# Four loads in flight, x of step 3 on the DMA crossbar and no last decay columns, in a fused HGRN2 and feed-forward kernel

## Chip, cores and metric

One core of a Trainium2 chip. The metric is the device time of one execution in microseconds (us). A kernel is run several times; an execution is called slow when it lies more than 1.5% above the fastest of its kernel, and comparisons use the fast ones. Times here vary by some 2 us from run to run, so small differences are read from ratios with their 95% interval. Different chips are not compared by their times. The granted clock is the share of TensorE's full clock that the chip granted: 1.0 is full, 0.5 half.

## The reference

```python
# q, k, v, f_logit: (batch 4, heads 8, seq 768, head_dim 48)
f = 1 / (1 + exp(-f_logit))
for t in range(768):
    state = f[:, :, t, :, None] * state + outer(k[:, :, t], v[:, :, t])
    y[:, :, t] = q[:, :, t] @ state
x = y.transpose(0, 2, 1, 3).reshape(3072, 384)
out = (maximum(x @ w_gate, 0) * (x @ w_val)) @ w_out     # d_ff = 1536
```

## The kernel before

The sequence is cut into 6 steps of 128 positions, numbered 0 to 5; each step has four batches, handled in two pairs. Every pair needs four loads of 384 KB (f, k, q, v). From f, ACT makes the logarithm of the gate (exp at L572, ln at L575), and TensorE (PE) sums it over positions with a triangular matrix, the **cumulative matmul** L582. What follows (exp, products, transposes, scores) gives y, which is the x of the feed-forward part. That part is a large heap of matmuls (L766, L789), used as filler wherever the attention part has nothing for PE.

The order of all this is not written down by hand. Every operation is entered in a plan with an assumed duration, and a list scheduler walks through assumed time and appends to one queue per engine. The queues are fixed when the kernel is built, and each engine works through its own strictly in order.

```python
flight = 3
first_xbar_x = 4
...
def load(n, c, b0, b1, after=(), ...):
    flow = 0.9 * (b1 - b0)          # assumed transfer time: 1.8 us for a pair
    op = add("SP", lambda: e.dma_start(dst, src), ..., after=after)
    dma(op, ..., flow, 2.0)         # assumed to land: flow + 2.0 us, plus backlog
...
# each load depends on the one `flight` places before it, in the plan
# and, as a semaphore wait for its landing, in the kernel
loads.append(load(n, c, b, b + load_batches, loads[-flight:][:1]))
...
def cum():                          # L582, and four one-column matmuls L584
    te.matmul(bc.ap[:, 0:HD], tri[:, :], bn[:, :, 0:D])
    for p in range(NP):             # decay columns, for the state update
        mm = te.matmul(bc.ap[:, HD + p:HD + p + 1], bn[...], ones[:, :])
...
if c < first_xbar_x:                # x transposed by PE (L699), copied by DVE (L703)
    chain("transpose_x", "PE", transpose_x, ..., occ=0.2)
else:                               # x transposed by a DMA on the SP queue (L707)
    op = add("SP", lambda: sy.dma_start(xT[...], xn[ni][:, :], transpose=True), ...)
```

## Time and profile before

| | before |
|---|---|
| time, median of 3 runs | 203.14 us (202.06 to 204.03) |
| profiled span | 201.4 us |
| granted TensorE clock, mean | 0.992 |
| last f landed / cumulative matmul started | 127.3 / 129.76 us |

Most of the profile's lines are in the prediction. Three more are needed for the comparison: groups of instructions of the kernel before that wait for a load. The columns are line, engine, operation, operands, count; busy us and mean ns; then the idle time of the engine just ahead of these instructions and what ended most of it.

```profile
L605 POOL TENSOR_TENSOR hats<-q_in,expo 128x384 bf16<-128x384 f32 x20 | 20.0, 1002 | 2.2 <-DMA q_in<-in_q_dram 2.2
L558 POOL CAST vpad<-v_in 128x384 bf16<-128x384 f32 x24 | 12.0, 515 | 3.0 <-DMA v_in<-in_v_dram 2.8
L572 ACT ACTIVATE f_in<-f_in 128x768 f32<-128x768 f32 x10 | 8.4, 838 | 6.4 <-DMA f_in<-in_f_logit_dram 6.4
```

ACT stood 6.4 us in all waiting for f, POOL 5 us for q and v. PE hid nearly all of that behind filler.

### The profile page before, as it was taken

What the parts mean: (1) busy time and instruction counts of PE and PEld (TensorE: products, weight loads), DVE (VectorE), ACT (ScalarE), POOL (GpSimd) and SP (SyncE); (2) the same over time, 40 slices, a digit from 0 to 9 for tenths busy, and PEclk for the clock granted to TensorE, in tenths of its full rate; (3) what the DMA queues carried; (4) which work ended last, traced back from release to release, by engine and by line L of the source; (5) the groups of instructions that cost most, each with busy time, mean ns of one, the idle gap of its engine ahead of it and who ended that gap; (6) DMA issues with size and microseconds to landing.
All of it is one profiled execution on the core that took longest, in us unless ns stands there. A gap on an engine that the chain in (4) does not pass through costs nothing.

```text
span 201.4 us, 4570 instructions
## 1 busy us (share of the span) xinstructions
PE 191.7 (95%) x1813; PEld 124.4 (62%) x1813; DVE 107.9 (54%) x212; ACT 115.2 (57%) x264; POOL 77.3 (38%) x111
## 2 busy tenths in 40 slices
PE   7989899799999999999999999599999999999995
PEld 5766688676789787855664655245555555444564
DVE  7268575565098988628586846135462334433210
ACT  2976868716678686877677572744354333443412
POOL 5189203563559687772858364053000000000000
PEclk9999999999999999999999999969999999999999
DMA  4999999999999999999989998979222001111113
GB/s 119 234 223 196 198 200 180 204 231 210 230 232 232 158 247 189 221 198 230 192 161 234 159 199 186 189 156 221 77 63 59 24 19 39 39 39 42 39 39 117
DMA packets 116660, 31.35 MB, mean 156 GB/s; under 512 B 109600, under 2 KB 116640, under 8 KB 116640
## 3 DMA queue, kind: packets, MB, share of 16 engines
q1 hardware_dynamic: 112656, 27.53, 67.2%
q0 software_dynamic: 3984, 3.54, 11.0%
q8 instruction: 14, 0.23, 0.5%
q14 instruction: 6, 0.05, 0.1%
HBM read 25.95 MB, written 4.72 MB: 152 GB/s over the span
## 4 chain that ended last, share of the span: by engine, by line
PE 73%; DMA 13%; SPq 8%; ACT 2%; POOL 2%; issue 1%; DVE 0%
PE ps L766 37%; PE ps L789 22%; SPq L399 7%; DMA q_in<-in_q_dram 4%; DMA wv<-in_moe_w_val_dram 4%; PE ps L638 3%; DMA f_in<-in_f_logit_dram 3%; DMA v_in<-in_v_dram 3%; PE ps L615 2%; PE ps L677 2%; PE ps L582 2%; PE ps L673 2%; PE ps L718 1%; PE ps L699 1%; PE ps L584 1%
## 5 line engine op out<-in xcount | busy, mean ns | idle before, releaser
L777 DVE TENSOR_TENSOR gT<-relu,ps 128x256 bf16<-128x256 bf16 (+1 forms) x96 | 52.2, 552 | 59.9 <-PE ps L766 37.2
L766 PE MATMUL ps<-xT,wg 128*128 128x256 bf16 (+1 forms) x288 | 63.1, 328 | 0.3 <-DMA wg<-in_moe_w_gate_dram 0.3
L773 ACT ACTIVATE relu<-ps 128x256 bf16<-128x256 f32 (+1 forms) x96 | 46.3, 490 | 29.1 <-PE ps L766 28.7
L766 PE MATMUL ps<-xT,wv 128*128 128x256 bf16 (+1 forms) x288 | 62.6, 326 | 0.0
L789 PE MATMUL ps<-wo,gT 128*128 128x384 bf16 (+2 forms) x300 | 52.5, 320 | 0.0
L789 PEld LDWEIGHTS ps<-wo,gT 128*128 128x128 bf16 x300 | 27.7, 98 | 17.4
L766 PEld LDWEIGHTS ps<-xT,wg 128*128 128x128 bf16 x288 | 27.0, 98 | 15.6 <-DMA wg<-in_moe_w_gate_dram 0.6
L644 DVE TENSOR_TENSOR ptm<-ps,tri 128x512 bf16<-128x512 f32 x48 | 30.6, 684 | 10.8 <-PE ps L638 10.7
L766 PEld LDWEIGHTS ps<-xT,wv 128*128 128x128 bf16 x288 | 26.1, 98 | 16.0 <-ACT relu L773 0.2
L809 ACT ACTIVATE osb<-ps 128x384 f32<-128x384 f32 (+2 forms) x25 | 11.8, 477 | 30.6 <-PE ps L789 30.5
L602 POOL TENSOR_TENSOR hats<-k_in,expo 128x384 bf16<-128x384 f32 x20 | 20.0, 1000 | 20.3 <-ACT expo L591 20.3
L605 POOL TENSOR_TENSOR hats<-q_in,expo 128x384 bf16<-128x384 f32 x20 | 20.0, 1002 | 2.2 <-DMA q_in<-in_q_dram 2.2
L734 POOL TENSOR_TENSOR st<-ssum,dec 128x384 bf16<-128x384 f32 x16 | 13.3, 830 | 16.2 <-DVE ssum L732 16.2
L455 PE MATMUL ps<-zeros 128*128 128x256 bf16 x89 | 13.0, 301 | 1.1 <-DVE zeros L359 1.1
L691 ACT ACTIVATE xn<-ps 128x384 bf16<-128x384 f32 x20 | 9.8, 488 | 7.1 <-PE ps L677 7.1
L558 POOL CAST vpad<-v_in 128x384 bf16<-128x384 f32 x24 | 12.0, 515 | 3.0 <-DMA v_in<-in_v_dram 2.8
L572 ACT ACTIVATE f_in<-f_in 128x768 f32<-128x768 f32 x10 | 8.4, 838 | 6.4 <-DMA f_in<-in_f_logit_dram 6.4
L591 ACT ACTIVATE expo<-ps 128x384 f32<-128x384 f32 x20 | 9.8, 492 | 3.0 <-PE ps L584 2.9
L455 PEld LDWEIGHTS ps<-zeros 128*128 128x128 bf16 x89 | 9.0, 107 | 3.0 <-DVE zeros L359 1.1
L638 PE MATMUL ps<-qkT 48*128 48x128 bf16 x192 | 8.9, 226 | 1.2 <-ACT qkT L528 0.8
L593 ACT ACTIVATE expo<-ps 128x384 f32<-128x384 f32 x20 | 10.0, 498 | 0.0
L732 DVE TENSOR_TENSOR ssum<-ps,st 128x384 f32<-128x384 f32 x16 | 8.8, 551 | 1.1 <-PE ps L718 0.9
(71 smaller groups left out, 158.3 us busy)
## 6 DMA issues: line engine op xcount, KB each, us to landing
out_dram<-osb SPq DMA_DIRECT2D x23, 192.0 KB, 2.2
f_in<-in_f_logit_dram SPq DMA_DIRECT2D x10, 384.0 KB, 6.2
k_in<-in_k_dram SPq DMA_DIRECT2D x10, 384.0 KB, 6.4
q_in<-in_q_dram SPq DMA_DIRECT2D x10, 384.0 KB, 4.5
v_in<-in_v_dram SPq DMA_DIRECT2D x10, 384.0 KB, 4.8
wg<-in_moe_w_gate_dram POOLq DMA_DIRECT2D x3, 384.0 KB, 7.1
wv<-in_moe_w_val_dram POOLq DMA_DIRECT2D x3, 384.0 KB, 7.4
wo<-in_moe_w_out_dram POOLq DMA_DIRECT2D x3, 384.0 KB, 7.2
```

Source lines behind the costliest of these rows:

```text
L399: op = add(eng, lambda: e.dma_start(dst, src), [], [f"{n}{c % NL}_{b}" for b in range(b0, b1)], occ=(0.8 if eng == "SP" else 0.3) * (b1 - ...
L455: op = add("PE", lambda: te.matmul(cold.ap[:, 0:256], zeros[:, 0:128], zeros[:, :]), ["zeros"], [cold], occ=0.22 if i < 17 else 0.11, lat= ...
L558: add("POOL", lambda: gp.tensor_copy(vout, vin[:, b, :, :].rearrange("p (n j) d -> p n j d", j=2)), [f"v{li}_{b}", f"vpad{vi}"], [f"v_{vi} ...
L602: add("POOL", lambda: gp.tensor_tensor(hk, kin[:, b, :, :], ex[:, 1, :].rearrange("p (h d) -> p h d", h=H), ALU.mult), [f"k{li}_{b}", f"ex ...
L605: add("POOL", lambda: gp.tensor_tensor(hq, qin[:, b, :, :], ex[:, 0, :].rearrange("p (h d) -> p h d", h=H), ALU.mult), [f"q{li}_{b}", f"ex ...
L638: mm = te.matmul(s.ap[:, p * C:(p + 1) * C], qkT[qi][lo:lo + D, 1, p, :], qkT[qi][lo:lo + D, 0, p, :])
L644: add("DVE", lambda j=j, s=s: ve.tensor_tensor(ptm[mi][:, j, :, :], s.ap[:, :].rearrange("p (n t) -> p n t", n=NP), mask, ALU.mult), [s, " ...
L734: add("POOL", lambda: gp.tensor_tensor(t4(s_new), t4(tmp), rate, ALU.mult), [key] + dk, [f"S{b}_{c % 2}"], prio=P + 8, **pool_t(HD))
L766: mm = te.matmul(bank.ap[:, 0:n], wt[:, kt, j * 128:(j + 1) * 128], xT[xi][:, kt, n0:n1], start=(kt == 0), stop=(kt == NK - 1))
L773: add("ACT", lambda: sc.activation(relu[ri][:, 0:n], gate.ap[:, 0:n], AF.Relu), [gate], [f"relu{ri}"], prio=P, **act_t(n))
L777: add("DVE", lambda: ve.tensor_tensor(gT[gi][:, j, n0:n1], relu[ri][:, 0:n], val.ap[:, 0:n], ALU.mult), [val, f"relu{ri}"], [f"gT{gi}_{j}_ ...
L789: mm = te.matmul(o.ap[:, 0:n1 - n0], gT[gi][:, j, b * C:(b + 1) * C], wo[:, j, n0:n1], start=(j == 0), stop=(j == NJ - 1))
```

## The change

Its intent: let a fourth load be queued so that DMA never pauses; take the x transposes of one more step off PE, the full engine, and give them to the DMA crossbar; drop matmuls whose result nobody reads in the last step. The core of the diff (new knobs for the stores, which keep their old setting, are cut):

```diff
-    flight = 3
+    flight = 4
...
-    first_xbar_x = 4
+    first_xbar_x = 3
...
-                te.matmul(bc.ap[:, 0:HD], tri[:, :], bn[:, :, 0:D])
-                for p in range(NP):
+                mm = te.matmul(bc.ap[:, 0:HD], tri[:, :], bn[:, :, 0:D])
+                for p in range(NP if c < NC - 1 else 0):
...
-            chain("cum", "PE", cum, ..., occ=0.29, lat=PE_L,
+            chain("cum", "PE", cum, ..., occ=0.29 - (0.12 if c == NC - 1 else 0), lat=PE_L,
```

In the changed kernel nearly all the lines named here have a number one higher (L582 becomes L583).

More of the change, by code (lines that the diff above doesn't have):

```diff
@@ L253, in bass_hgrn2_outer__then__ffn_reglu_kernel @@
     n_tiled = 1
-    first_xbar_x = 4
+    first_xbar_x = 3
     load_batches = 2
     hat_engines = ['DVE', 'POOL']
+    STORE = 'SP'
     TAIL = [0, 256, 384]
@@ L586, in cum @@
                 return mm
-            chain("cum", "PE", cum, ["tri", "ones", f"bneg{bi}", f"bn{bi}_{bj}"], [bc], occ=0.29, lat=PE_L,
+            chain("cum", "PE", cum, ["tri", "ones", f"bneg{bi}", f"bn{bi}_{bj}"], [bc], occ=0.29 - (0.12 if c == NC - 1 else 0), lat=PE_L,
                 prio=P, opens=[bc])
@@ L811, in ffn_out @@
             dst = bass.AP(tensor=out.tensor, offset=(b * S + g * C) * DM + n0, ap=[[DM, C], [1, n1 - n0]])
-            op = add("SP", lambda dst=dst, oi=oi, n0=n0, n1=n1: sy.dma_start(dst, osb[oi][:, n0:n1]), [f"osb{oi}_{x}" for x in TAIL[:-1] if n0 <= x < n1], [f"out{g}_{b}_{n0}"],
-                     occ=0.2, lat=0.9, prio=P)
+            op = add(STORE, lambda dst=dst, oi=oi, n0=n0, n1=n1: (sy if STORE == "SP" else sc).dma_start(dst, osb[oi][:, n0:n1]), [f"osb{oi}_{x}" for x in TAIL[:-1] if n0 <= x < n1], [f"out{g}_{b}_{n0}"],
+                     follows=first_stores if g == 0 else [], occ=0.2 if STORE == "SP" else 0.4, lat=0.9 if STORE == "SP" else 1.2, prio=P)
             dma(op, f"osb{oi}_{n0}", 0.45 * (n1 - n0) / DM)
+    first_stores = [tails["loadSP"]] if '0' == "1" else []
     OJ = 4
@@ L864, in bass_hgrn2_outer__then__ffn_reglu_kernel @@
             op.val = n
-    stores = [op for op in order["SP"] if op.writes and op.writes[0].startswith("out")]
+    stores = [op for op in order[STORE] if op.writes and isinstance(op.writes[0], str) and op.writes[0].startswith("out")]
     def run(name, eng):
```

## The prediction

> **What bounds the kernel now.** I read the page first, then the chain that ended last in order of time, the timeline of TensorE (PE) and of the SP queue, and the SP queue's own waits.
>
> ```profile
> PE 191.7 (95%) x1813; PEld 124.4 (62%) x1813; DVE 107.9 (54%) x212; ACT 115.2 (57%) x264; POOL 77.3 (38%) x111
> PE   7989899799999999999999999599999999999995
> PEclk9999999999999999999999999969999999999999
> DMA  4999999999999999999989998979222001111113
> ```
>
> PE is full except for one slice (126 to 131 us); the next slices show a lowered clock. The DMA engines are full up to about 140 us and nearly idle after. So there are two regimes: up to 140 us loads and PE run neck and neck, and after it PE alone works off the feed-forward backlog. PE executes in order, so whatever it loses before 140 us is added to the end. The chain says what it lost:
>
> ```profile
> 119.42 1.22 SPq L812
> 120.68 1.19 SPq L707
> 121.92 5.33 DMA f_in<-in_f_logit_dram
> 127.27 0.84 ACT f_in L572
> ...
> 128.98 0.74 ACT bneg L575
> 129.76 0.34 PE ps L582
> ```
>
> This is f of the last step, second batch pair. It is issued behind a store and an x transpose, takes 5.33 us, and ACT needs 2.5 us from landing until the cumulative matmul L582 may start. PE's timeline shows the price:
>
> ```profile
> 126.76 0.81 PE L789 MATMUL ps<-wo,gT 128*128 128x384 bf16 x4
> 129.76 0.34 PE L582 MATMUL ps<-bneg,tri 128*128 128x384 bf16 x1 [2.19 <-ACT bneg L575]
> ...
> 131.99 1.44 PE L766 MATMUL ps<-xT,wg 128*128 128x512 bf16 x3
> ...
> 135.73 0.81 PE L766 MATMUL ps<-xT,wv 128*128 128x512 bf16 x3
> ```
>
> 2.2 us idle, and then the same three matmuls take 1.44 instead of 0.81 us. The table of windows gives a granted clock of 0.50 for 131.2 to 134.5, so about 1.65 us more are lost. Together 3.85 us is what better loading could win here.
>
> **What the Trainium skill says.** (1) "TensorE: Matmul & The Clock Gate", section "What's actually happening": the clock is at half or full speed, decided by a free-running window of about 3.4 us; an idle one halves it. The trace agrees in size (0.50 for some 3.3 us), though here the idle part was only 2.2 us. (2) Same page, "Back-to-back issue gap": N/2.4 + 2.5 ns for a warm matmul. For N = 128 that is 56 ns; the three L699 transposes below start 0.17 us before the next group: it agrees. (3) "Advanced Engine Details and Errata", "X-Bar Transpose (TRN2)": transposes by DMA are as fast as regular DMAs. This trace disagrees for the queue: an unobstructed x transpose of 96 KB holds SP for 1.24 us, a load of 384 KB for 0.45.
>
> ```profile
> 62.53 0.33 PE L699 MATMUL ps<-ident,xn 128*128 128x128 bf16 x3
> 62.70 0.49 PE L766 MATMUL ps<-xT,wv 128*128 128x256 bf16 x3
> ```
> ```profile
> 130.35 0.45 SPq L399 DMA_DIRECT2D q_in<-in_q_dram  x1
> 143.15 2.48 SPq L707 DMA_TRANSPOSE xT<-xn  x2
> ```
>
> **The change part by part.**
>
> Decay columns: 4 works x 4 one-column matmuls L584 go. A group of four takes 0.10 us from its start to the next group's (51.66 to 51.77), so 4 x 0.10 = 0.4 us of PE.
>
> x of step 3: 4 groups of L699 go, 4 x 0.17 = 0.7 us of PE, and four DVE copies L703 of 0.354 us, which are off the path. Sum on PE: **1.1 us**, certain. In exchange four DMA transposes enter the SP queue while it is contended.
>
> Flight: the load that stands `flight` places earlier is handed over as a true dependency, so each load waits for that one to land. What three in flight cost is in the SP queue's waits:
>
> ```profile
> SPq L399 <- DMA v_in<-in_v_dram: 0.5, 1, 0.5
> SPq L399 <- DMA q_in<-in_q_dram: 0.4, 1, 0.4
> SPq L399 <- DMA k_in<-in_k_dram: 0.4, 1, 0.4
> ```
>
> 1.3 us in all, near 64 to 70 us. After 76 us loads wait for no such landing. They take 1.5 to 2.9 us to issue when others are ahead: the queue is held by the transfers, not by the count. A fourth load cannot add bandwidth that is used up (222 GB/s in 50 to 76 us, DMA share 1.08; 193 in 76 to 127, share 1.02).
>
> But flight also changes the **planned order**, since the kernel's scheduler believes that loads come sooner. I summed the PE instructions ahead of each step's first L582 in both programs, from the start-to-start times of the timeline (0.216 us for 512 columns, 0.109 for 256, 0.163 for 384, 0.041 for a score and so on). The sum reproduces the trace before with a steady offset of about 7 us. In the new order PE is at these points earlier: step 3 second pair at 80.2 us (85.9 before), step 4 at 88.6 and 99.8 (95.6, 105.0), step 5 at 110.2 and 121.7 (116.0, and 127.5 where PE came to stand). So filler was moved behind, and f would have to come as much earlier. Landings of f before (issue plus time to landing in the DMA view): 79.5, 90.5, 102.6, 113.2, 127.3; plus 2.5 us for ACT that is 82.0, 93.0, 105.1, 115.7, 129.8. Spare time there was 3.9, 2.5, 0, 0.3 and -2.3 us. To be free of stalls f must now land 1.7, 4.4, 5.3, 5.5 and **8** us sooner.
>
> Will it? Between the first f of step 2 (landed at 54.1) and the last f (127.3) the SP order before has 28 loads, 8 qkT transposes, 7 stores and 1 x transpose. Mean spacing of landings: load 2.04, qkT 1.34, store 0.72, x 0.47 us; sum 57.1 + 10.7 + 5.0 + 0.5 = 73.3, as measured (73.2). In the new order the first f goes out 2.4 us sooner, ahead of two stores, and lands 1.4 sooner by my estimate (52.7). After it come 28 loads, 8 qkT, 8 stores and 4 x transposes: 57.1 + 10.7 + 5.8 + 4 x (0.5 to 1.24) = 75.6 to 78.6. Less 1 to 3 us for waits that go (the 1.3 above, and pauses of SP for stores and for a transpose whose input was late), the last f lands at 125.5 to 130, about 127.5: no sooner than now. L582 then starts near 130.
>
> From there PE has, by the same sums, 72.0 us of work in the new order against 67.7 before (the difference is the moved filler). It ends at 130 + 72.0 = 202.0, against 199.06 before, plus perhaps half of another clock drop (0.85): **+2.9 to +3.8 us**, so 206 to 207.
>
> **The rivals.**
>
> *Loads do come sooner.* For it: SP is in order, and a load behind a store or behind a wait for three landings starts late; DMA falls to 9 to 17 GB/s for about half a us near 69 and 78 us, where a fourth load might already be queued. Against it: in those moments SP was still issuing the load before. If the last f lands 4 us sooner (123.5), L582 starts at 126, PE ends at 198 with little clock loss, 1 us better: about 201.5. With all stalls gone it is 1.1 + 3.85 = 5 us, 198.2, which is the floor and needs f at 119.
>
> *SP becomes the bound.* Transposes in a row hold SP for 1.2 to 1.3 us each while the loads already queued drain in 2 us each. For it: the new order has a cluster of four (qkT, qkT, x, x) ahead of the first f of step 5, and two pairs between it and the last f. Then f lands at 130 to 131, PE ends at 205 with a clock drop: 208 to 209.
>
> *Only the deletions count.* PE still stalls 2 us somewhere and the change yields its 1.1 us: 202. That would need the reordering to be neutral, which the 5 us of lost spare time speak against.
>
> **Range and chances.** Main line 206 (weight about 0.5), loads sooner 201.5 (0.25), deletions only 202 (0.1), SP bound 208.5 (0.15): 103 + 50.4 + 20.2 + 31.3 = 204.9; I say **204.6**, since the main line's size rests on mean spacings. The range is 200.4 to 208.4, from the good rival less its noise to the bad one; the three runs before spread over 2 us. Faster by over 2% means under 199.1, nearly the floor: 0.08. Slower by over 2% means above 207.2: 0.23. Within 2%: 0.69.
>
> **What would show it right or wrong.** Right: PE idle before L582 in steps 4 and 5 grows from 2.2 us to some 6 to 8 us in several pieces, released by ACT's bneg; the last f lands between 125 and 130; granted clock dips more than once; L699 has 24 matmuls, L584 64; the stretch after the last stall is dense and about 72 us long. Wrong: the last f lands by 123 us, with SP's load issues following each other more closely than 2 us, or PE's idle time before L582 stays near 2 us.

## The result, and the profile after

| | before | after |
|---|---|---|
| median of 6 runs, same chip | 203.58 us | 209.19 us |
| lowest to highest | 202.06 to 204.84 | 207.44 to 211.78 |
| profiled span | 201.4 us | 207.1 us |
| PE idle or at half clock, over the whole span (see below) | 11.2 us | 18.0 us |
| granted clock, mean | 0.992 | 1.0 |
| last f landed | 127.3 us | 128.95 us |

The ratio is **1.027** (1.020 to 1.034): slower. A ratio here is the mean time of one kernel's fast runs over that of the other's in the same rounds, so it is not quite the ratio of the medians quoted.

The page of the changed kernel, busy shares and slices (40 slices of 5.2 us, tenths; no clock row is printed, since this trace holds no clock records, and its 1.0 stands for that; the matmuls show that the clock did not fall: from 40 us on every 512-column one takes 0.38 to 0.39 us, where before some took 0.63):

```profile
PE 191.0 (92%) x1785; PEld 122.8 (59%) x1785; DVE 106.2 (51%) x208; ACT 115.2 (56%) x264; POOL 77.1 (37%) x111
PE   7979899969999998979897879979999999999995
DMA  5999999999999998999997699999232111111113
```

PE's one hole of before has become a row of shallow ones from 40 to 140 us; after that PE is as dense as before. The same groups as above, now with long waits:

```profile
L606 POOL TENSOR_TENSOR hats<-q_in,expo 128x384 bf16<-128x384 f32 x20 | 19.9, 1000 | 9.3 <-DMA q_in<-in_q_dram 8.3
L559 POOL CAST vpad<-v_in 128x384 bf16<-128x384 f32 x24 | 12.1, 513 | 12.7 <-DMA v_in<-in_v_dram 12.6
L573 ACT ACTIVATE f_in<-f_in 128x768 f32<-128x768 f32 x10 | 8.4, 843 | 11.9 <-DMA f_in<-in_f_logit_dram 11.8
```

Each load-consuming group waits longer: f 11.8 us instead of 6.4, v 12.6 instead of 2.8, q 8.3 instead of 2.2. For f the landings are hardly later. f of step 3 second pair, step 4, step 5 landed at 79.5, 90.5, 102.6, 113.2, 127.3 us before and 80.1, 90.2, 102.3, 115.7, 128.95 after. So for f ACT **asks sooner**, and the data does not come sooner. In step 5 k, q and v do come later, by 3 to 6 us: the two q at 125.4 and 140.1 instead of 119.1 and 134.8, the two v at 127.4 and 143.6 instead of 122.3 and 138.3. All 8.3 us of waits for q stand there. So in the last step of this trace the two causes, earlier asking and later loads, are mixed; the experiments have to part them.

How that reaches PE: PE's waits of the changed kernel (line, what it waited for: us in total, times, longest):

```profile
PE ps L719 <- POOL vpad L559: 3.1, 2, 1.8
PE ps L639 <- DMA qkT<-hats: 2.8, 2, 1.5
PE ps L583 <- ACT bneg L576: 1.5, 2, 1.1
...
PE ps L767 <- ACT relu L774: 0.9, 1, 0.9
PE ps L790 <- ACT relu L774: 0.9, 1, 0.9
```

Before there were two such waits of over 1.2 us, now there are many of about one. Some name relu, an operation of the feed-forward part that needs no load. ACT's timeline around one of them (start, duration, operation, idle before and releaser) and PE's of the same moment:

```profile
102.36 0.84 ACT L573 ACTIVATE f_in<-f_in 128x768 f32<-128x768 f32 x1 [2.23 <-DMA f_in<-in_f_logit_dram]
103.11 0.58 ACT L774 ACTIVATE relu<-ps 128x512 bf16<-128x512 f32 x1
```
```profile
103.74 0.82 PE L767 MATMUL ps<-xT,wv 128*128 128x512 bf16 x3 [0.93 <-ACT relu L774]
```

ACT works through its queue in order. It stands 2.23 us for f; the relu queued behind it could have run long before, its matmuls having ended by about 101.4 us. PE's next filler group waits for just this relu, and stands too. A late load stops the filler that was meant to hide it.

The SP queue of the changed kernel from 103.7 us (start, duration of the issue, operation, count):

```profile
103.72 3.63 SPq L625 DMA_TRANSPOSE qkT<-hats  x2
107.39 2.56 SPq L708 DMA_TRANSPOSE xT<-xn  x2
110.00 0.58 SPq L400 DMA_DIRECT2D v_in<-in_v_dram  x1
110.62 1.31 SPq L400 DMA_DIRECT2D f_in<-in_f_logit_dram  x1
```

Four transposes in a row; v and f of the next work wait 6.3 us for their turn. In 110 to 120 us the DMA share falls to 0.79. The next f landed at 115.7 instead of 113.2.

**The account.** I took PE's actual start times less the summed start-to-start times of the instructions ahead; what is left over is stall and half clock. PE's work fell from 187.66 to 186.57 us (-1.1), stall and half clock rose from 11.2 to 18.0 (+6.8). Sum +5.7, the difference of the spans. The largest pieces after 45 us: 2.0 at v (45.9; before, 1.7 at q, 40.5), 1.0 and 1.1 at relu (81.4 and 103.7 us), 1.2 at bneg (92.3), 1.5 at v (114.5), 1.4 and 1.7 at qkT (123.3 and 137.0). The half clock of before (1.65) is gone.

### The profile page after: what moved, and what is told of

Read it like the earlier page. It is cut to its first block, busy times and chain, and to the rows that moved or that the text cites. A ratio compares the mean times of both kernels' runs of the same rounds, so it can differ in the third digit from the quotient of the medians.

```text
span 207.1 us, 4513 instructions
## 1 busy us (share of the span) xinstructions
PE 191.0 (92%) x1785; PEld 122.8 (59%) x1785; DVE 106.2 (51%) x208; ACT 115.2 (56%) x264; POOL 77.1 (37%) x111
## 3 DMA queue, kind: packets, MB, share of 16 engines
q1 hardware_dynamic: 114320, 27.93, 64.8%
## 4 chain that ended last, share of the span: by engine, by line
PE 40%; DMA 26%; SPq 15%; ACT 7%; POOL 7%; issue 3%; POOLq 0%
PE ps L767 20%; PE ps L790 16%; DMA v_in<-in_v_dram 14%; SPq L400 12%; DMA f_in<-in_f_logit_dram 7%; DMA wv<-in_moe_w_val_dram 3%; SPq L625 3%; DMA qkT<-hats 2%; POOL hats L606 2%; POOL vpad L559 2%; ACT f_in L573 2%; ACT bneg L576 2%; POOL st L735 2%; ACT relu L774 2%; POOL hats L603 1%
## 5 line engine op out<-in xcount | busy, mean ns | idle before, releaser
L790 PE MATMUL ps<-wo,gT 128*128 128x384 bf16 (+2 forms) x300 | 51.9, 319 | 0.9 <-ACT relu L774 0.9
L767 PEld LDWEIGHTS ps<-xT,wv 128*128 128x128 bf16 x288 | 27.0, 98 | 18.9 <-ACT relu L774 1.4
L810 ACT ACTIVATE osb<-ps 128x384 f32<-128x384 f32 (+2 forms) x25 | 11.8, 476 | 29.0 <-PE ps L790 29.0
L559 POOL CAST vpad<-v_in 128x384 bf16<-128x384 f32 x24 | 12.1, 513 | 12.7 <-DMA v_in<-in_v_dram 12.6
L573 ACT ACTIVATE f_in<-f_in 128x768 f32<-128x768 f32 x10 | 8.4, 843 | 11.9 <-DMA f_in<-in_f_logit_dram 11.8
L592 ACT ACTIVATE expo<-ps 128x384 f32<-128x384 f32 x20 | 9.9, 496 | 5.3 <-PE ps L585 5.2
L639 PEld LDWEIGHTS ps<-qkT 48*128 48x128 bf16 x192 | 5.5, 94 | 7.8 <-issue 3.1
```

Source lines behind the costliest of these rows:

```text
L559: add("POOL", lambda: gp.tensor_copy(vout, vin[:, b, :, :].rearrange("p (n j) d -> p n j d", j=2)), [f"v{li}_{b}", f"vpad{vi}"], [f"v_{vi} ...
L639: mm = te.matmul(s.ap[:, p * C:(p + 1) * C], qkT[qi][lo:lo + D, 1, p, :], qkT[qi][lo:lo + D, 0, p, :])
L767: mm = te.matmul(bank.ap[:, 0:n], wt[:, kt, j * 128:(j + 1) * 128], xT[xi][:, kt, n0:n1], start=(kt == 0), stop=(kt == NK - 1))
L790: mm = te.matmul(o.ap[:, 0:n1 - n0], gT[gi][:, j, b * C:(b + 1) * C], wo[:, j, n0:n1], start=(j == 0), stop=(j == NJ - 1))
```

## The experiments

Theory: the order that the scheduler makes when it believes in four loads in flight is the cause. It moves filler from ahead of each step to behind it, by 5 to 7 us, while transfers cannot come sooner. Rivals: the count in flight itself (queue contention), or the x transposes that hold SP and delay loads. All runs are in 5 rounds against the kernel before on the same chip: e1 to e4 on one chip (before 202.93), e5 to e8 on a second (203.67), e9 to e12 on a third (200.39).

| run | what it is | median us | ratio to before (95%) |
|---|---|---|---|
| e1_flight4_only | before, flight 4 | 209.34 | 1.030 (1.025 to 1.035) |
| e2_xbar3_only | before, x of step 3 on crossbar | 208.08, mostly slow runs | 1.007 (1.000 to 1.015) |
| e3_decay_only | before, no last decay columns | 204.26 | 1.002 (0.996 to 1.008) |
| e4_order3_wait4 | before's order, waits as with 4 | 203.72 | 1.002 (0.997 to 1.007) |
| e5_order4_wait3 | e1's order, waits as with 3 | 209.64 | 1.027 (1.022 to 1.032) |
| e6_after_flow12 | after, slower loads assumed (1.2 a batch) | 209.08 | 1.027 (1.022 to 1.032) |
| e7_f4_x4_flow11 | flight 4, x on PE, no decay, 1.1 | **201.23** | **0.989** (0.984 to 0.994) |
| e8_f3_x4_flow10 | flight 3, x on PE, no decay, 1.0 | **201.35** | **0.988** (0.984 to 0.993) |
| e9_flow12_copy | e6, plain copies for x of step 3 | 208.40 | 1.042 (1.037 to 1.047) |
| e10_xbar3_copy | e2, plain copies for x of step 3 | 202.79 | 1.016 (1.011 to 1.021) |
| e11_f4_x4_flow10 | e7 with 1.0 | 202.37 | 1.011 (1.005 to 1.017) |
| e12_after_x_on_pe | after, x of step 3 on PE | 207.12 | 1.033 (1.027 to 1.039) |

### Each part alone

```diff
# e1                      # e2                        # e3: only the hunk of cum()
-    flight = 3           -    first_xbar_x = 4
+    flight = 4           +    first_xbar_x = 3
```

> The kernel before with flight = 4 alone. Order theory (the scheduler believes that loads come sooner, so filler is moved behind the attention work and in-order PE and ACT stand waiting): the last pair's first cumulative matmul now has only 110.8 us of PE work ahead of it (120.0 before, 114.6 in the changed kernel) and 76.8 us behind it; the last f should still land at 126 to 129 us, so PE ends at about 129 + 2.5 + 76.8 = 208 and the run is 3 to 4% slower than before, worse than the whole change. Rival A (the x transposes that crowd the SP queue and the DMA engines are the cause): no x transposes are added here, so it should be within 1% of before. Rival B (four loads really in flight slow each other): slower by about 2.5%, with longer times from issue to landing and the last f landing later than 129 us.

> The kernel before with x of step 3 on the crossbar alone (flight 3). Order theory: the last pair's first cumulative matmul has 120.6 us of PE work ahead (120.0 before), so PE is not asked for f sooner; six x transposes stand ahead of the last f instead of one, which costs the landing 2.5 to 5 us by spacing (0.5 to 1.1 us each), and PE work falls by 0.7 us: within 1.5% of before, with a longer idle time at that one place. Rival A: slower by 2 to 3%, as the whole change. Rival B: as before, within 1%.

> The kernel before without the decay columns of the last step. All theories: 16 one-column matmuls less, 0.4 us of PE work at a place where PE bounds the end; order otherwise unchanged. Ratio 0.998 +- 0.005: the interval will hold 1.

Flight alone costs as much as the whole change. And here the last f did land sooner, by 5.5 us (121.75; I had expected 126 to 129), but it was asked for sooner still. So that the ratio came as expected is in part luck: the expectation's sum put the end of PE at 208 us, it was 205.3, and 4.2 us of that are waits and half clock after the last pair's cumulative matmul, which the sum does not have. ACT's and PE's timeline of e1:

```profile
121.77 0.84 ACT L572 ACTIVATE f_in<-f_in 128x768 f32<-128x768 f32 x1 [3.06 <-DMA f_in<-in_f_logit_dram]
```
```profile
132.60 0.62 PE L638 MATMUL ps<-qkT 48*128 48x128 bf16 x16 [1.90 <-DMA qkT<-hats]
133.16 1.46 PE L766 MATMUL ps<-xT,wv 128*128 128x512 bf16 x3
```

ACT idles 3 us for this f, then PE 1.9 us for the transposed q and k of the next work, and three matmuls take 1.46 us at half clock. The moved filler is done at the end, when nothing is left to hide. By my sums PE has 76.8 us of work after the last pair's first cumulative matmul in e1, 67.7 before, 72.0 after. This answers the prediction's rival "loads do come sooner": they may, and the time still rises.

e2 is the least clean run: four of its six executions were slow, and its trace is of a slow one (208.34 us). In that trace the x transposes hold PE up (stall before the feed-forward matmul of step 3, shown below); its two fast runs show +0.7%, with an interval that touches zero. e3 shows nothing measurable; the 0.4 us that the prediction gave it lies within the interval. Its edit is not a deletion alone, as I had expected: the shorter assumed duration (0.17 instead of 0.29 us) also changed the order of PE, ACT and DVE in the last step.

### Order and count, taken apart

The dependency does two things: it shapes the plan, and it is a wait at run time. In e4 the plan is made with 3 and, once the order is fixed, each load is set to wait for the landing of the load four before. In e5 it is the other way round.

```diff
# e4, after the scheduling (e5: flight = 4, and i - 3)
+    for i, op in enumerate(loads):
+        for d in [d for d in op.deps if d in loads and op.deps[d] == "raw"]:
+            if i >= n_early:
+                del op.deps[d]
+        if i >= n_early:
+            op.deps[loads[i - 4]] = "raw"
```

> The instruction order of the kernel before, every engine, to the instruction, but at run time each load waits for the load four places earlier instead of three. Order theory: the count in flight itself matters little, only the 1.3 us of waits near 64 to 70 us go; ratio 0.99 to 1.00, last f lands at 125.5 to 127.5 us (127.3 before). Rival A: the same, 1.00. Rival B: slower by 2 to 3%.

> The instruction order of e1 (scheduled with flight 4, which was 3.0% slower than before), but at run time each load waits for the load three places earlier, as before. Order theory: as slow as e1, ratio 1.025 to 1.040. If what made e1 slow is the fourth load really in flight: ratio near 1.00.

This is the cleanest pair: in the traces the instructions of PE, ACT, DVE, POOL and SP stand in e4 in the very order of before, in e5 in that of e1. The order alone costs 2.7%; the count alone nothing (1.002), though in e4 no load waits for another any more (1.3 us before). The pair moves the order as a whole; that the moved filler is the part that matters is argued from the traces of e1 and, below, of e7 and e8. PE's main wait in e4 is that of before, at the same place and of the same size:

```profile
PE ps L582 <- ACT bneg L575: 2.3, 1, 2.3
```

The last f landed at 128.2 us in e4, 127.3 before, and the first cumulative matmul of all also started 0.85 us later (7.82, 6.97): a fourth queued load brought nothing sooner. The trace of e5 fell in a slow run and is not used.

### A scheduler that believes less

If belief is the fault, telling the scheduler a longer transfer should mend it. In the trace before, the mean time from the landing ahead of it to a load's own is 2.04 us in the middle of the kernel; the plan assumed 1.8.

```diff
# e6: changed kernel, 1.2     # e7: flight 4, x on PE, no decay, 1.1
-        flow = 0.9 * (b1 - b0)  # e8: flight 3, x on PE, no decay, 1.0
+        flow = 1.2 * (b1 - b0)  # e11: as e7, 1.0
```

> The changed kernel whole, except that its scheduler is told that a load holds the DMA engines for 1.2 us a batch instead of 0.9 (2.4 us a load, the measured spacing being about 2.0). No instruction is added or taken away but warm-up matmuls. Order theory: PE work ahead of the last pair's first cumulative matmul grows from 114.6 to 119.2 us, and of the earlier ones by 4 to 12 us; the waits of PE for bneg, relu and v shrink from 18.0 us in all (start included) to 11 to 13 us, and the run is level with before, ratio 0.99 to 1.01. Rival A (x transposes on the queue are the cause): still slower than before by 2% or more, since four x transposes still stand ahead of the last f.

> Flight 4, x of step 3 on PE as before, no decay columns in the last step, scheduler told 1.1 us a batch. PE work ahead of the last pair's cumulative matmul 122.8 us, behind it 64.8. Order theory: no stall over 1 us after 45 us, PE ends near 187.7 + 7 to 9 = 195 to 197, ratio 0.97 to 0.99. Rival (four in flight harm): slower than before.

> Flight 3, x of step 3 on PE, no decay columns in the last step, scheduler told 1.0 us a batch instead of 0.9. PE work ahead of the last pair's cumulative matmul 122.6 us, behind it 64.8. Order theory: the 2.2 us stall before that matmul and the half clock after it go, ratio 0.975 to 0.99; the level of e7 to within 1%, whatever the flight.

> As e7 but the scheduler is told 1.0 us a batch instead of 1.1 (e1 has 0.9 and was 3.0% slower, e7 1.1% faster). Work ahead of the last pair's cumulative matmul 117.7 us (110.8 in e1, 122.8 in e7). Order theory: a dose in between: f should land near 123 us, PE asks near 117.7 + 7 = 125 and gets it near 126, so stalls of 1 to 3 us in all; ratio 0.99 to 1.01. If order were not what matters: no trend between the three.

e7 and e8 are about 1.1% **faster than the kernel before**, and their intervals do not touch 1; they are the best versions found, on one chip. e7's page and its last f:

```profile
PE 191.5 (97%) x1801; PEld 125.0 (63%) x1801; DVE 107.7 (54%) x212; ACT 116.6 (59%) x264; POOL 76.4 (39%) x111
```
```profile
126.34 0.84 ACT L572 ACTIVATE f_in<-f_in 128x768 f32<-128x768 f32 x1
```

This f had landed at 123.4, 3 us before ACT came to it, and there is no idle time in the brackets' place. From 45 us on PE has no stall of over 1 us. The last pair's first cumulative matmul in e7 and in e8:

```profile
130.95 0.32 PE L582 MATMUL ps<-bneg,tri 128*128 128x384 bf16 x1
131.83 0.34 PE L582 MATMUL ps<-bneg,tri 128*128 128x384 bf16 x1 [1.41 <-ACT bneg L575]
```

Both start later than before (129.76), and in e8 the last f came at 130.0 and PE still waits 1.4 us for it, which I had expected to go. Yet PE ends at 195.9 and 196.8 instead of 199.0: only 64.8 us of work stand behind this matmul, against 67.7 before (and 1.65 of half clock) and 76.8 in e1. When a load lands says little without the work that is left behind it.

With four in flight the ratio goes 1.030 (0.9 assumed, e1), 1.011 (1.0, e11; 0.99 to 1.01 was expected), 0.989 (1.1, e7). But the three ran on three chips, and the kernel before differs between these by up to 3.3 us in the median, three times the 1.1 us between e11 and e7. So the step from e11 to e7 is not shown. In e11's trace PE does not wait for the last f either; it loses 2.6 us at the scores of the last pairs (L638, at 137.4 and 143.1), and the profile does not tell to what. e8 (three, 1.0) and e7 (four, 1.1) do equally well, but they differ in two knobs; for the count at run time, e4 is the test.

**e6 failed**: I expected 0.99 to 1.01, and it stayed at 1.027. PE's timeline of e6:

```profile
114.49 0.62 PE L639 MATMUL ps<-qkT 48*128 48x128 bf16 x16
119.33 0.50 PE L719 MATMUL ps<-vpad,hats 128*128 128x96 bf16 x4 [4.22 <-POOL vpad L559]
```

One wait of over 4 us, followed by half clock. In this order only some 1.2 us of PE work lies between the cumulative matmuls of step 4's second pair (113.80) and its state matmul, while the work on POOL between them takes 4.5 us without a pause (two products with k, two with q, the first cast of v, 114.8 to 119.3). No load is late there. So a longer assumed transfer is no cure as such: this order has a hole of another kind.

### The x transposes

e9 and e10 replace the crossbar transposes of step 3 by plain copies of the same bytes. Their outputs are wrong, which doesn't matter for the times. e12 puts x of step 3 back on PE in the changed kernel.

```diff
# e9 on e6, e10 on e2                                  # e12 on after
-  sy.dma_start(xT[...], xn[ni][:, :], transpose=True)  -    first_xbar_x = 3
+  sy.dma_start(xT[...], xn[ni][:, :].rearrange(        +    first_xbar_x = 4
+      "p (n t) -> p n t", n=NK))        # c == 3 only
```

> The kernel of e6, same order on every engine, with the four x tiles of step 3 moved by a plain copy of the same 96 KB in place of the transpose (the result is wrong on purpose). Theory 'transposes hold the SP queue': a copy holds it some 0.4 us against 1.25, so the loads behind go out sooner; the last f lands at 124 to 128 us instead of 132.1, the 4.4 us stall for v near 119 us shrinks below 1.5 us, ratio 0.99 to 1.01 instead of 1.027. Rival (the x tiles cost transfer time on the DMA engines, whatever their kind; or e6 is slow by its order alone): ratio stays at 1.02 to 1.03 and the last f at 131 us or later.

> The kernel of e2 (flight 3, x of step 3 by crossbar), same order, with the four x tiles of step 3 moved by a plain copy (wrong result on purpose). Theory 'transposes hold the SP queue': the 2.8 us stall at the first feed-forward matmul of step 3 near 117 us goes, the last f lands at 126 to 129 us instead of 133.7, and the median falls from 208.1 to 202 to 204 us. Rival: median stays at 207 to 208.5.

> The changed kernel with x of step 3 back on PE (flight 4 and no decay columns stay). Order theory: as e1, work ahead of the last cumulative matmul 110.6 us, so no better than the changed kernel although no x transpose stands ahead of the last f: ratio to before 1.025 to 1.035. Rival A alone (x transposes are the one cause): ratio within 1% of 1.00.

The copies do what was expected of the queue: in e9 three of the four hold SP for 0.62 to 0.66 us, where an unobstructed transpose holds it for 1.25 (the fourth, behind a load, takes 1.51), and the last f landed at 128.1 instead of 132.1 us (0.8 of this is an earlier start of the whole); in e10 at 129.9 instead of 133.7, e2's trace being of a slow run. PE's timeline of e2, of that slow run, at the feed-forward matmul that needs the transposed x:

```profile
117.38 1.46 PE L766 MATMUL ps<-xT,wg 128*128 128x512 bf16 x3 [2.63 <-DMA xT<-xn]
```

In e10 the longest wait for an x is 1.0 us:

```profile
PE ps L767 <- DMA xT<-xn: 1.0, 1, 1.0
```

So the transposes delay loads; that they delay filler stands in a slow run alone. In time this is not shown: e9 is no better than e6, because the wait that POOL causes stays (PE's timeline of e9):

```profile
118.44 0.50 PE L720 MATMUL ps<-vpad,hats 128*128 128x96 bf16 x4 [3.89 <-POOL vpad L559]
```

In its trace e9 also ran 10.2 us at half clock, e6 6.8. I had expected 0.99 to 1.01, so e9 failed too. And e10's ratio (1.016) is not below e2's (1.007), which rests on two fast runs of another chip. What part of e2's loss is the crossbar and what part its order stays **open**.

e12 is clear: with x of step 3 on PE again the change still costs 3.3%. The last f came at 121.9 us instead of 128.95, and it did not help: ACT's queue asked for it 3.4 us before it came. So the transposes are not needed for the loss; that they add nothing to it is not shown, since with them the order is another.

## Why the prediction was wrong

It said 204.6 (200.4 to 208.4), with 0.69 for no difference; it is 209.19, slower, outside the range.

**Right: the mechanism.** That SP is held by the transfers and not by the count: e4. That flight works through the planned order (e1, e5), and that moved filler comes back at the end (e1's trace). That the last f lands at 125.5 to 130, no sooner than before: 128.95. PE's removed work, 1.1 us: measured 1.1.

**Wrong: how the main line was sized.** The step that failed is the sum 130 + 72.0 = 202.0 for the end of PE, which leaves no wait after the last f. Actually L583 started at 131.09, and PE ended at 204.80: 1.1 us from the later f and 1.7 us from a wait for the last transposed q and k at 137 us. The prediction had only the f of each pair as a cause of waits. v (1.5 at 114.5) and qkT (1.4 and 1.7) each cost as much as an f; part of that is asking sooner, part the later k, q and v of step 5, in shares that no run shows. The 0.85 us for another clock drop did not come: the clock stayed full. Main line 206 to 207; the mechanism as such made about 209.

**Held: the term "4 x (0.5 to 1.24)" for the x transposes.** The prediction's sum starts where the first f of step 2 lands. From there to the last f the changed kernel took 75.0 us (53.9 to 128.95), within its 75.6 to 78.6 less 1 to 3; e1 took 69.25 (52.5 to 121.75), with one qkT and four x less in this stretch. Less 1.34 for the qkT, that leaves about 1.1 us for each x, an estimate from two traces. What was off is the start: the first f was to land at 52.7 and came at 53.9, and so the last f came at the late side of its range. The rival **SP becomes the bound** (0.15, 208 to 209) came partly true: four transposes in a row ahead of f of step 5, as it said, 2.5 us delay there, and k, q and v of step 5 3 to 6 us later. Its number is the nearest, but its f at 130 to 131 and its clock drop did not come, and e12 shows that it was not needed for the loss.

**Wrong: the weights.** The main line said 206 to 207. Averaging it with "loads come sooner" (201.5) and "deletions only" (202) made 204.6. (By its own figures, 1.06 us less than 203.14, the first of these stands at 202.1; that would move the average by 0.15.) The first rival took a sooner f for a gain, against the prediction's own reckoning that f must land 8 us sooner to be free of stalls; e1 got 5.5 and was 3% slower. The second was named as contrary to the lost spare time, and still got 0.1. Without the two the point would have stood at 206 or above.

**Signs.** "6 to 8 us in several pieces, released by bneg": PE idled 10 us after 45 us in several pieces, most released by relu, v and qkT; only 1.5 us by bneg. It was overlooked that ACT's wait for f also holds relu, which stands behind it in the same queue. "Clock dips more than once": never in the profiled run. "The stretch after the last stall about 72 us": 73.7 from L583, with the wait at 137 in it.

## What to carry to other kernels

Where a static scheduler fixes the order, a parameter that promises sooner data is a change of order first: compare how much work stands ahead of each consumer before and after, and ask whether the transfers can follow, for every load and not only for the one that hurts today. An engine that works through its queue in order passes a late load on to work that does not need it, so filler behind a wait is no filler. Two orders with a longer assumed load time gained 1.1% here (e7, e8), where adding loads in flight lost 2.7%; but each order has to be run: e11, with the value nearest to the measured spacing and four in flight, lost 1.1%, and e6 made a new hole.

## What the Trainium skill lacked or had wrong

- "TensorE: Matmul & The Clock Gate", section "What's actually happening", gives half clock after an idle window of about 3.4 us. Less idle time was enough here. In the eleven traces that hold clock records (slow runs among them) every change of the clock lies on a grid of 3.41 us. PE lost its full clock after seven windows of this grid, those in which it idled 1.79 us or more, and kept it after all 614 in which it idled 1.68 us or less. The kernel before waited 2.2 us, of which 2.04 lay in one window, and then had a clock of 0.50 for 3.4 us; e4 waited 2.3 us at the same place, 1.08 in one window and 1.22 in the next, and kept 1.0. So whether a wait of about 2 us costs half clock was decided by where it fell. This is read from these traces; no run tests it by itself.
- "Advanced Engine Details and Errata", section "X-Bar Transpose (TRN2)", calls transposes as fast as regular DMAs, and says nothing of the issuing queue. There they are not: 1.25 us for an unobstructed x transpose, 0.62 to 0.66 for a plain copy of the same bytes (e9), 0.45 for a load of four times as many.
- On "DMA: Bandwidth & Descriptors" I found nothing on how long an issue holds its queue when transfers are ahead of it. Here, in the changed kernel after 45 us, a load's issue took either 0.43 to 0.59 us or, behind others, 1.3 to 3.0 us, and waiting for the third or the fourth load before made no difference (e4, 1.002).
